# Attention scores in packed units of four blocks, one more half batch of x through the crossbar, and a longer wait for the loads

## Chip, core and metric

The kernel runs on one core of a Trainium2 chip. The metric is the time of one execution on the device, in microseconds (us); the median of several runs is given. A profile is one more execution, recorded by the hardware profiler; its span runs from the first instruction to the last.

## What is computed

Two parts follow each other. First an attention with 4 batches, 8 heads, 768 positions and 64 elements a head: each position attends to the first 8 positions and to the 96 positions up to itself, with a penalty that grows with the distance (a slope for each head). Then a feed-forward layer over the 4 x 768 = 3072 tokens with 512 features: a product with `w_in` (512 x 2048), a squared ReLU, a product with `w_out` (2048 x 512).

```python
scores = scale * (q @ k.T) - slope[h] * dist          # only kept positions
a = exp(scores - max) ; a = a / sum(a)
x = (a @ v), heads side by side -> [3072, 512]
out = (relu(x @ w_in) ** 2) @ w_out
```

Since only 8 + 96 positions are kept, a tile of 128 queries needs two blocks of 128 keys at most: its own tile, and a "before" block. In the before block the first 32 key rows are replaced by those of tile 0, so that the global positions are in it (`kb` for keys, `vb` for values, both copied together on the chip). The weights exp(score) are multiplied by a mask that holds exp(-slope * distance), or 0; the sum comes from a column of ones at the end of v.

## The kernel before

**Tiles and halves.** A batch has 6 tiles of 128 queries. Work goes by half batches (`hb` 0 to 7) of three tiles: `half` 0 holds tiles 0 to 2, `half` 1 tiles 3 to 5. Heads go in pairs (`NPAIR` = 4): the two heads of a pair lie on partitions 0-63 and 64-127, so their score matmuls (L453, 64 rows each) run side by side. The first two half batches (the opening) are handled tile by tile in an order written out by hand; their code is touched only in which buffers they share.

**Stages.** From then on TensorE works through stages, one for each half batch: stage `hb` runs the feed-forward of half batch `hb` as *main* work (layer 1: 16 jobs of 4 matmuls, L563; layer 2: 12 jobs of 4 matmuls, L612; 28 in all) and slips in the attention of half batch `hb` + 1 as *side* work. Stage 1 is shorter: its main work is 18 layer-2 jobs. `merge` puts each side job ahead of the main job with the number that it is given.

**Attention of a half batch, before.** For each pair of heads `a`: `score` (one job, 10 or 12 matmuls into four PSUM banks of 384 or 256 columns: `GROUPS`, two banks for each head), exponentials on ScalarE (L468), products with the mask on VectorE (L480, L484) into `phat`, then `attend` (L508, phat times v into PSUM bank `av`), normalization on VectorE (L515, L517) into `tm`, and the transpose of `tm` into `xt`, the input of layer 1. For half batch 2, q and k are turned by TensorE (`turn`, L400) and x too (`to_x`, L532, with an eviction on ScalarE or VectorE). For half batches 3 to 7 q, k (`turn_by_dma`, L418) and x (`to_x_by_dma`, L544) are transposed by crossbar DMAs that SP issues.

**Banks.** [...] Six (`ps_big`) serve scores, layer 1 and layer 2 in turn, two (`ps_att`) attention outputs and transposes.

**Order.** A planner (`Plan.run`) fixes the order of the instructions on each engine before the kernel runs, from costs and latencies written in the code. TensorE's jobs keep the order in which they were listed, the loads keep theirs, and the rest goes by the planned time. On the chip each engine then takes its list strictly in order: an instruction that waits holds up what stands behind it.

**Loads.** q, k and v come from memory by DMAs that POOL issues (L310), in one list: q, k, v of a half batch, three tiles each. The q load of half batch `hb` > 3 waits for the q and k transposes of half batches `hb` - 2 (their staging buffers become free) and `hb` - 1 (so that loads and those transposes don't meet). The q and k transposes of a half batch wait for its last k load.

```python
before = (prev.turned if prev else []) + (halves[x.hb - 1].turned if x.hb > 3 else [])
```

Of the kernel before, what the change touches and what calls it, by code (L numbers as in the profile page):

```python
# [25 lines left out]
LOADING = """v1 k1 v0 q1 k2 q2 k3 v2 k4 q3 q4 c0 k5 q5 v3 c1 v4 c2 c3 v5"""  # L26

# [121 lines left out]
def kernel(  # L149
# [150 lines left out]
    def list_loads(x):  # L300
        r0 = x.half * HALF
        prev = halves[x.hb - 2] if x.hb >= 2 else None
        before = (prev.turned if prev else []) + (halves[x.hb - 1].turned if x.hb > 3 else [])
        vbefore = [halves[x.hb - x.half - 3].attended[-1]] if x.hb >= 4 else []

        def rows(src, name, t, rank=None):
            def emit(e):
# [4 lines left out]
                if x.hb > 3 and name == "sq" and t == 0:  # L312
                    for turn in halves[x.hb - 1].turns:
                        behind(dma, turn)
# [98 lines left out]
    def turn_by_dma(x):  # L413
# [16 lines left out]
    GROUPS = {  # L430
        0: ([(0, 0), (1, 0), (1, 1)], [(2, 0), (2, 1)]),
        1: ([(3, 0), (4, 0), (5, 0)], [(3, 1), (4, 1), (5, 1)]),
    }

    def score(x, a, only=None):
        groups = GROUPS[x.half]
        st, weighs = x.phat.setdefault(a, ({}, []))
        mine = [g for g in range(2) if only in (None, g)]

        def emit(e):  # L440
            bt = x.bt
            for g in mine:
                blocks = groups[g]
                st[g] = pair = [ps_big.tile([P, 512], FP32, name="sp", tag="big")
                                for _ in range(2)]
                if g == mine[0]:
                    warm(pair[0])
                for i, (r, before) in enumerate(blocks):
                    for h in range(2):
                        rows = slice(h * D, (h + 1) * D)  # L450
                        lhsT = (bt.kb[rows, a, r - 2, :] if before and r > 1
                                else bt.qk[rows, 1, r - before, a, :])
                        nc.tensor.matmul(pair[h][:, i * P:(i + 1) * P], lhsT=lhsT,  # L453
                                         rhs=bt.qk[rows, 0, r, a, :],
                                         start=True, stop=True)
        n_mm = sum(len(groups[g]) for g in mine)
        job = plan.pe(0.182 + 0.062 * n_mm, emit, x.qk_ops[a], [big] * 2 * len(mine))

        for i, g in enumerate(mine):
            blocks = groups[g]  # L460
            n = len(blocks) * P
            c0 = 3 * P * g
            exps = []
            for h in range(2):
                def ex(e, g=g, h=h, n=n):
                    if h == 0:
                        st["ex", g] = phat_p.tile([P, 2, 3 * P], FP16, name="ex", tag="ex", bufs=6)
# [55 lines left out]
    def to_x(x, a):  # L523
        st, norm = x.tm[a]

        def emit(e):
            if x.xt is None:
                x.xt = h_p.tile([P, NCT, HALF], FP16, name="xt", tag="xt")
# [373 lines left out]
```

## Time and profile before

| what | value |
|---|---|
| median of 5 runs | 218.9 us (218.71, 218.89, 218.90, 219.59, 219.90) |
| the profiled execution: its time, its span | 219.5 us, 217.7 us |
| busy: TensorE, ScalarE, VectorE | 96%, 58%, 54% of the span |
| score matmuls L453 | 264, in 24 jobs |
| attention matmuls L508 | 264, in 24 jobs |
| transposes of x on TensorE L532 | 12 |
| crossbar transposes of x L544 | 20 |
| granted TensorE clock | 0.999 of full speed |

How to read it: in rows of groups, a line of the code, the engine, the operation, `out<-in` by the program's names, shapes, the number of instructions; then busy time, the mean of one in ns, and the idle time just before them with what ended it. In a timeline a row is start, length (both us), engine, line and operation; idle time in brackets. PE is TensorE, PEld its weight loads, DVE VectorE, ACT ScalarE, POOL GpSimd, SP SyncE; SPq and POOLq are the queues of these engines that issue DMAs. `hps` is layer 1's sum, `yps` layer 2's, `sp` the scores, `av` the attention output, `ex` the exponentials, `hr` the relu and `h` its square. The ends of matmuls are modelled, so the starts are what counts.

### The profile page before, as it was taken

The numbers are of one execution on the slowest core, as the hardware profiler recorded it, in microseconds if no ns is written. First come the engines' busy times: TensorE is split into PE (matmuls) and PEld (weight loads), VectorE is DVE, ScalarE is ACT, GpSimd is POOL, SyncE is SP. The second block draws the span as 40 slices with busy tenths as digits, with TensorE's granted clock in tenths as the row PEclk, the third lists the DMA queues.
The fourth block names the chain that finished last, engine by engine and source line by source line (L and its number), as shares of the span: only waits on it lengthen the run. The fifth ranks groups of instructions, "written<-read, shape, count | busy, mean of one in ns | idle before, by whom it ended". The sixth has DMA issues, their size and how long they took to land.

```text
span 217.7 us, 4847 instructions
## 1 busy us (share of the span) xinstructions
PE 210.1 (96%) x1917; PEld 127.8 (59%) x1917; DVE 117.5 (54%) x339; ACT 127.1 (58%) x286; POOL 68.2 (31%) x84
## 2 busy tenths in 40 slices
PE   6998999999999999999999999999999999999993
PEld 7776899755555565446554565446644565455552
DVE  7488887434764298317952488308850488114300
ACT  7689986744662788139831787149821885137421
POOL 8996534486049019204900193000000000000000
PEclk9999999999999999999999999999999999999999
DMA  7999999999999979997994899673103101220012
GB/s 117 150 159 179 196 200 207 168 154 173 97 205 159 174 186 103 145 201 133 126 132 121 188 94 144 105 147 96 39 20 114 53 18 36 69 96 0 3 52 93
DMA packets 106727, 26.41 MB, mean 121 GB/s; under 512 B 99408, under 2 KB 103760, under 8 KB 106704
## 3 DMA queue, kind: packets, MB, share of 16 engines
q0 software_dynamic: 77024, 13.37, 84.5%
q1 hardware_dynamic: 28640, 12.46, 24.8%
q10 hardware_dynamic: 1040, 0.26, 0.5%
q8 instruction: 15, 0.25, 0.5%
q14 instruction: 8, 0.07, 0.1%
HBM read 27.26 MB, written 6.29 MB: 154 GB/s over the span
## 4 chain that ended last, share of the span: by engine, by line
PE 74%; DMA 12%; POOL 10%; issue 1%; DVE 1%; ACT 0%; SPq 0%; POOLq 0%
PE hps L563 36%; PE yps L612 27%; DMA v<-in_v_dram 6%; POOL sk L310 4%; PE av L508 4%; DMA w_in_sb<-in_moe_w_in_dram 4%; POOL sq L310 4%; PE sp L453 3%; POOL v L310 2%; DMA qk<-sk 2%; PE yps L640 2%; PE av L740 1%; PE sp L701 1%; PE trx L767 0%; DVE phat L484 0%
## 5 line engine op out<-in xcount | busy, mean ns | idle before, releaser
L563 PE MATMUL hps<-xt,w_in_sb 128*128 128x384 f16 (+2 forms) x608 | 89.1, 301 | 0.6 <-DMA w_in_sb<-in_moe_w_in_dram 0.6
L612 PE MATMUL yps<-w_out_sb,h 128*128 128x512 f16 x368 | 83.0, 379 | 0.0
L563 PEld LDWEIGHTS <-w_in_sb 128*128 128x128 f16 x608 | 53.7, 98 | 27.3 <-DMA w_in_sb<-in_moe_w_in_dram 0.8
L598 DVE TENSOR_TENSOR h<-hr 128x768 f16<-128x768 f16 (+1 forms) x70 | 36.1, 521 | 52.5 <-ACT hr L587 52.1
L587 ACT ACTIVATE hr<-hps 128x384 f16<-128x384 f32 (+1 forms) x110 | 55.5, 514 | 14.8 <-PE hps L563 11.8
L612 PEld LDWEIGHTS <-h 128*128 128x128 f16 x368 | 35.1, 98 | 39.4
L198 ACT COPY y<-yps 128x512 f32<-128x512 f32 (+1 forms) x25 | 14.3, 570 | 62.8 <-PE yps L612 60.3
L468 ACT ACTIVATE ex<-sp 128x384 f16<-128x384 f32 x96 | 36.7, 477 | 1.5 <-PE sp L453 1.4
L310 POOL DMA_DIRECT2D sq<-in_q_dram x23 | 20.4, 895 | 52.3 <-DMA qk<-sq 28.2
L310 POOL DMA_DIRECT2D v<-in_v_dram x24 | 21.8, 934 | 5.6 <-DMA w_out_sb<-in_moe_w_out_dram 3.3
L310 POOL DMA_DIRECT2D sk<-in_k_dram x23 | 20.5, 906 | 3.7 <-DMA w_out_sb<-in_moe_w_out_dram 2.9
L517 DVE TENSOR_TENSOR tm<-av,rec 128x384 f16<-128x384 f32 x24 | 13.4, 557 | 0.8
L200 DVE COPY vb<-v 128x520 f16<-128x520 f16 (+1 forms) x32 | 10.2, 321 | 5.6 <-DMA v<-in_v_dram 5.1
L515 DVE RECIPROCAL rec<-av 128x6 f32<-128x6 f32 x24 | 4.7, 196 | 14.8 <-PE av L508 14.5
L508 PEld LDWEIGHTS <-phat 128*128 128x128 f16 x264 | 10.0, 98 | 3.8 <-DVE phat L484 0.6
L484 DVE TENSOR_TENSOR phat<-ex,mask 128x768 f16<-128x768 f16 x24 | 12.2, 550 | 0.0
L508 PE MATMUL av<-v,phat 128*128 128x65 f16 x168 | 11.5, 194 | 0.0
L200 DVE COPY kb<-qk 128x96 f16<-128x96 f16 (+4 forms) x56 | 11.0, 266 | 0.8 <-DMA qk<-sk 0.5
L480 DVE TENSOR_TENSOR phat<-ex,mask 128x768 f16<-128x768 f16 (+1 forms) x24 | 10.6, 485 | 0.1
L508 PE MATMUL av<-vb,phat 128*128 128x65 f16 x96 | 10.2, 194 | 0.3 <-DVE phat L484 0.3
L453 PE MATMUL sp<-qk 64*128 64x128 f16 x168 | 8.9, 219 | 0.0
L200 DVE COPY qk<-trp 128x512 f16<-128x512 f16 (+1 forms) x11 | 4.3, 398 | 8.3 <-PE trp L400 4.8
(65 smaller groups left out, 135.3 us busy)
## 6 DMA issues: line engine op xcount, KB each, us to landing
out_dram<-y SPq DMA_DIRECT2D x23, 256.0 KB, 2.3
v<-in_v_dram POOLq DMA_DIRECT2D x24, 128.0 KB, 6.6
sk<-in_k_dram POOLq DMA_DIRECT2D x23, 128.0 KB, 5.8
sq<-in_q_dram POOLq DMA_DIRECT2D x23, 128.0 KB, 5.6
w_in_sb<-in_moe_w_in_dram POOLq DMA_DIRECT2D x4, 512.0 KB, 10.9
w_out_sb<-in_moe_w_out_dram POOLq DMA_DIRECT2D x4, 512.0 KB, 15.8
xt<-tm SPq DMA_TRANSPOSE x20, 3.1
rsk<-in_k_dram ACTq DMA_DIRECT2D x1, 256.0 KB, 4.3
```

Of the source, the lines that this page charges most:

```text
L198: nc.scalar.copy(out=out, in_=in_)
L200: eng(e).tensor_copy(out=out, in_=in_)
L310: dma = nc.gpsimd.dma_start(out=dst, in_=src[x.b, :, r0 + t * P:r0 + (t + 1) * P, :] .rearrange("h p d -> p h d"))
L453: nc.tensor.matmul(pair[h][:, i * P:(i + 1) * P], lhsT=lhsT, rhs=bt.qk[rows, 0, r, a, :], start=True, stop=True)
L468: nc.scalar.activation(out=st["ex", g][:, h, 0:n], in_=st[g][h][:, 0:n], func=AF.Exp, scale=scale)
L484: eng(e).tensor_tensor(out=phat[:, :, c0:c0 + n].rearrange("p e (i c) -> p e i c", c=P), in0=ex[:, :, 0:n].rearrange("p e (i c) -> p e i c ...
L508: nc.tensor.matmul(av[:, h, j, :], lhsT=phat[:, h, c * P:(c + 1) * P], rhs=rhs, start=n == 0, stop=n == len(mine) - 1)
L517: nc.vector.tensor_tensor(out=st["tm"].rearrange("p t e d -> p e t d"), in0=av[:, :, :, 0:D], in1=rec[:, :, :, None].to_broadcast([P, 2, H ...
L563: nc.tensor.matmul(st["ps"][:, i * n:(i + 1) * n], lhsT=w_in_sb[:, kk, m * P:(m + 1) * P], rhs=x.xt[:, kk, c0:c1], start=kk == 0, stop=kk ...
L587: nc.scalar.activation(out=o, in_=i, func=AF.Relu)
L598: eng(e).tensor_tensor(out=x.h2[:, m0:m0 + width, c0:c1], in0=hr, in1=hr, op=ALU.mult)
L612: nc.tensor.matmul(st["ps"], lhsT=x.h2[:, m, j * P:(j + 1) * P], rhs=w_out_sb[:, m, :], start=m == 0, stop=m == NFT - 1)
```

## The change

1. *Scores in units of four blocks.* A block is (pair of heads, tile, own or before). Four blocks of one head side fill a whole PSUM bank (4 x 128 columns), so a unit takes two banks and two exponentials of 512 columns. An even half batch has 5 units: one for each pair (tiles 1 and 2, own and before), and one with tile 0 of all four pairs, whose product goes into a tile of its own (`phat0`). An odd one has 24 blocks in a row, cut into 6 units, so a unit can reach over two pairs. `TOGETHER` joins the units into three TensorE jobs of two units (the last of an even half batch: one). The weights lie as `phat[pair][head, tile, own|before]`.
2. *Places.* `PLACES` names the main job ahead of which each side job goes: three score jobs, four attend jobs, and for half batch 2 its four `turn` jobs. Scores now begin at place 0, ahead of the first layer-1 job, where before the fractions gave place 2; `merge` takes the numbers as they are.
3. *x of half batch 2 by crossbar.* `to_x` is gone, and `to_x_by_dma` serves every half batch from 2 on. It also records its DMAs in `x.turns`.
4. *Loads.* The loads of half batch `hb` > 3 wait also for the last x transpose of half batch `hb` - 2.
5. The opening's `ex` and `ph0` tiles share buffers with those of the later half batches.

```diff
@@ -24,6 +24,12 @@
 
 
...
+PLACES = {2: (3, 7, 7, 7, 10, 11, 12, 1, 0, 1, 0),
+          0: (0, 4, 9, 6, 11, 16, 18), 1: (0, 6, 11, 9, 11, 17, 19)}
 
 
 class Op:
@@ -300,7 +306,7 @@
     def list_loads(x):
         r0 = x.half * HALF
         prev = halves[x.hb - 2] if x.hb >= 2 else None
-        before = (prev.turned if prev else []) + (halves[x.hb - 1].turned if x.hb > 3 else [])
+        before = (prev.turned if prev else []) + ([*halves[x.hb - 1].turned, prev.x_ops[NPAIR - 1]] if x.hb > 3 else [])
         vbefore = [halves[x.hb - x.half - 3].attended[-1]] if x.hb >= 4 else []
 
         def rows(src, name, t, rank=None):
@@ -310,7 +316,7 @@
                 dma = nc.gpsimd.dma_start(out=dst, in_=src[x.b, :, r0 + t * P:r0 + (t + 1) * P, :]
                                           .rearrange("h p d -> p h d"))
                 if x.hb > 3 and name == "sq" and t == 0:
-                    for turn in halves[x.hb - 1].turns:
+                    for turn in halves[x.hb - 1].turns + halves[x.hb - 2].turns[-1:]:
                         behind(dma, turn)
                 if name == "sk":
                     x.last_load = dma
@@ -427,87 +433,90 @@
         for a in range(NPAIR):
             x.qk_ops[a] = x.turned + [plan.add(*fix_k(x, a), x.turned[:1], wait=4.0)]
 
-    GROUPS = {
-        0: ([(0, 0), (1, 0), (1, 1)], [(2, 0), (2, 1)]),
-        1: ([(3, 0), (4, 0), (5, 0)], [(3, 1), (4, 1), (5, 1)]),
-    }
-
-    def score(x, a, only=None):
-        groups = GROUPS[x.half]
-        st, weighs = x.phat.setdefault(a, ({}, []))
-        mine = [g for g in range(2) if only in (None, g)]
-
-        def emit(e):
-            bt = x.bt
-            for g in mine:
-                blocks = groups[g]
-                st[g] = pair = [ps_big.tile([P, 512], FP32, name="sp", tag="big")
-                                for _ in range(2)]
-                if g == mine[0]:
-                    warm(pair[0])
-                for i, (r, before) in enumerate(blocks):
+    UNITS = [[[(a, r, bf) for r in range(1, HT) for bf in (False, True)] for a in range(NPAIR)]
+             + [[(a, 0, False) for a in range(NPAIR)]]]
+    seq = [(a, r, bf) for a in range(NPAIR) for r in range(HT, NT) for bf in (False, True)]
+    UNITS.append([seq[i:i + 4] for i in range(0, len(seq), 4)])
+    TOGETHER = [[[0, NPAIR], [1, 2], [3]], [[0, 1], [2, 3], [4, 5]]]
+
+    def score(x, k):
+        bt = x.bt
+        units = [UNITS[x.half][u] for u in TOGETHER[x.half][k]]
+        sp = {}
+
+        def emit(e):
+            for u, unit in enumerate(units):
+                sp[u] = [ps_big.tile([P, 4, P], FP32, name="sp", tag="big") for _ in range(2)]
+                if u == 0:
+                    warm(sp[u][0].rearrange("p i c -> p (i c)"))
+                for i, (a, r, before) in enumerate(unit):
                     for h in range(2):
                         rows = slice(h * D, (h + 1) * D)
                         lhsT = (bt.kb[rows, a, r - 2, :] if before and r > 1
                                 else bt.qk[rows, 1, r - before, a, :])
-                        nc.tensor.matmul(pair[h][:, i * P:(i + 1) * P], lhsT=lhsT,
-                                         rhs=bt.qk[rows, 0, r, a, :],
-                                         start=True, stop=True)
-        n_mm = sum(len(groups[g]) for g in mine)
-        job = plan.pe(0.182 + 0.062 * n_mm, emit, x.qk_ops[a], [big] * 2 * len(mine))
-
...
-            weighs.append(plan.add({"DVE": 0.06 + n * 0.0011}, weigh,
-                                   exps + [mask_ops[2 * a], mask_ops[2 * a + 1]]))
+                        nc.tensor.matmul(sp[u][h][:, i, :], lhsT=lhsT,
+                                         rhs=bt.qk[rows, 0, r, a, :], start=True, stop=True)
+        pairs = sorted({a for unit in units for a, _, _ in unit})
+        job = plan.pe(0.182 + 0.062 * 4 * len(units), emit,
+                      [o for a in pairs for o in x.qk_ops[a]], [big] * 2 * len(units))
+        for u, unit in enumerate(units):
+            weigh_unit(x, unit, job, u, sp)
+
+    def weigh_unit(x, unit, job, u, sp):
+        st = {}
+        exps = []
+        for h in range(2):
+            def exp(e, h=h):
+                if h == 0:
+                    st["ex"] = phat_p.tile([P, 2, 4, P], FP16, name="ex", tag="ex", bufs=6)
+                nc.scalar.activation(out=st["ex"][:, h], in_=sp[u][h], func=AF.Exp, scale=scale)
+            exps.append(plan.add({"ACT": 0.505}, exp, [job] + exps))
+            job.users[2 * u + h].append(exps[-1])
+        if unit[0][1] == 0:
+            def weigh(e):
+                x.phat0 = phat_p.tile([P, 2, NPAIR, P], FP16, name="ph0", tag="ph0")
+                eng(e).tensor_tensor(
+                    out=x.phat0, in0=st["ex"], op=ALU.mult,
+                    in1=mask[:, :, 0:P].rearrange("p (a h) c -> p h a c", h=2))
+            op = plan.add({"DVE": 0.62}, weigh, exps + mask_ops)
+            for a in range(NPAIR):
+                x.weighs[a].append(op)
+            return
+        for a in sorted({a for a, _, _ in unit}):
+            mine = [(i, r) for i, (b, r, _) in enumerate(unit) if b == a][::2]
+            i0, n, t0 = mine[0][0], len(mine), mine[0][1] % HT
+
+            def weigh(e, a=a, i0=i0, n=n, t0=t0):
+                if a not in x.phat:
+                    x.phat[a] = phat_p.tile([P, 2, HT, 2 * P], FP16, name="phat", tag="phat")
+                eng(e).tensor_tensor(
+                    out=x.phat[a][:, :, t0:t0 + n], op=ALU.mult,
+                    in0=st["ex"][:, :, i0:i0 + 2 * n].rearrange("p e (t b) c -> p e t (b c)", b=2),
+                    in1=mask[:, 2 * a:2 * a + 2, None, P:3 * P].to_broadcast([P, 2, n, 2 * P]))
+            x.weighs[a].append(plan.add({"DVE": 0.06 + n * 0.28}, weigh,
+                                        exps + mask_ops[2 * a:2 * a + 2]))
 
     def attend(x, a):
         bt = x.bt
-        st, weighs = x.phat[a]
-        where = [(3 * g + i, r, bf) for g, blocks in enumerate(GROUPS[x.half])
-                 for i, (r, bf) in enumerate(blocks)]
-
-        def emit(e):
-            phat = st["phat"]
+        st = {}
+        blocks = [(j, bf) for j in range(HT) for bf in (False, True) if x.half or j or not bf]
+
+        def emit(e):
             st["av"] = av = ps_att.tile([P, 2, HT, D + 1], FP32, name="av", tag="att")
             warm(av.rearrange("p e t d -> p (e t d)"))
             for h in range(2):
-                for j in range(HT):
+                for j, before in blocks:
                     r = x.half * HT + j
-                    mine = [(c, bf) for c, rr, bf in where if rr == r]
-                    for n, (c, before) in enumerate(mine):
-                        rhs = (bt.vb[:, r - 2, 2 * a + h, :] if before and r > 1
-                               else bt.v[:, r - before, 2 * a + h, :])
-                        nc.tensor.matmul(av[:, h, j, :], lhsT=phat[:, h, c * P:(c + 1) * P],
-                                         rhs=rhs, start=n == 0, stop=n == len(mine) - 1)
-        job = plan.pe(0.0305 * 2 * len(where), emit, weighs + x.v_in + [bt.vb_ops[t] for t in range(*tiles_before(x))], [att])
+                    rhs = (bt.vb[:, r - 2, 2 * a + h, :] if before and r > 1
+                           else bt.v[:, r - before, 2 * a + h, :])
+                    lhsT = (x.phat[a][:, h, j, before * P:(before + 1) * P] if r
+                            else x.phat0[:, h, a, :])
+                    nc.tensor.matmul(av[:, h, j, :], lhsT=lhsT, rhs=rhs, start=not before,
+                                     stop=before or r == 0)
+        job = plan.pe(0.0305 * 2 * len(blocks), emit, x.weighs[a] + x.v_in
+                      + [bt.vb_ops[t] for t in range(*tiles_before(x))], [att])
 
         def norm(e):
             av = st["av"]
@@ -520,30 +529,15 @@
         x.attended.append(job)
         x.tm[a] = (st, plan.after(job, {"DVE": 0.74}, norm))
 
-    def to_x(x, a):
+    def to_x_by_dma(x, a):
         st, norm = x.tm[a]
 
         def emit(e):
             if x.xt is None:
                 x.xt = h_p.tile([P, NCT, HALF], FP16, name="xt", tag="xt")
-            st["trx"] = ps_att.tile([P, HT, P], FP16, name="trx", tag="att")
-            warm(st["trx"].rearrange("p t c -> p (t c)"))
-            for t in range(HT):
-                nc.tensor.transpose(out=st["trx"][:, t, :], in_=st["tm"][:, t, :, :],
-                                    identity=ident)
-        job = plan.pe(3 * 0.056, emit, [norm], [att])
-        x.x_ops[a] = plan.after(job, {"ACT": 0.39, "DVE": 0.31}, lambda e: copy(
-            e, x.xt[:, a, :], st["trx"].rearrange("p t c -> p (t c)")))
-
-    def to_x_by_dma(x, a):
-        st, norm = x.tm[a]
-
-        def emit(e):
-            if x.xt is None:
-                x.xt = h_p.tile([P, NCT, HALF], FP16, name="xt", tag="xt")
-            nc.sync.dma_start_transpose(
+            x.turns.append(nc.sync.dma_start_transpose(
                 out=x.xt[:, a, :].rearrange("p (t c) -> p t c", c=P),
-                in_=st["tm"].rearrange("p t e d -> p (t e d)"))
+                in_=st["tm"].rearrange("p t e d -> p (t e d)")))
         x.x_ops[a] = plan.add({"SP": 1.2}, emit, [norm])
         x.x_ops[a].lag = 2.5
 
@@ -650,6 +644,7 @@
 
     for x in halves:
         x.turned, x.turns, x.attended = [], [], []
+        x.weighs = [[] for _ in range(NPAIR)]
         x.qk_ops, x.phat, x.tm, x.x_ops, x.h2_ops, x.l1, x.l2 = {}, {}, {}, {}, {}, {}, {}
         x.xt = x.h2 = None
 
@@ -705,12 +700,12 @@
             needs += [kb_ops[r - 1]] if r > 1 else tile_ops[r - 1]
         job = plan.pe(0.182 + NPAIR * 0.07 + added * H * 0.056, emit, needs, [big] * 2)
         exps = []
-        st["ph", before] = phat_p.tile([P, 2, NPAIR, P], FP16, name="ph0", tag="ph0", bufs=4)
+        st["ph", before] = phat_p.tile([P, 2, NPAIR, P], FP16, name="ph0", tag="ph0")
         for h in range(2):
             def ex(e, h=h):
                 if h == 0 and not added:
-                    st["ex", before] = phat_p.tile([P, 2, NPAIR, P], FP16, name="ex0", tag="ex0",
-                                                   bufs=3)
+                    st["ex", before] = phat_p.tile([P, 2, NPAIR, P], FP16, name="ex", tag="ex",
+                                                   bufs=6)
                 nc.scalar.activation(out=st["ph" if added else "ex", before][:, h],
                                      in_=st["sp", before][h], func=AF.Exp, scale=scale)
             exps.append(plan.add({"ACT": 0.51}, ex, [job] + exps))
@@ -775,21 +770,19 @@
 
     def attention(x):
         jobs = []
-        early = x.hb > 2
+        places = PLACES[x.hb if x.hb == 2 else x.half]
+        for k in range(len(TOGETHER[x.half])):
+            jobs.append((places[k], lambda k=k: score(x, k)))
         for a in range(NPAIR):
-            at = 0.04 + 0.16 * a if early else 0.1 + 0.17 * a
-            jobs.append((at, lambda a=a: score(x, a)))
-            jobs.append((at + 0.17, lambda a=a: attend(x, a)))
-            if early:
-                jobs.append((at + 0.17, lambda a=a: to_x_by_dma(x, a)))
-            else:
-                jobs.append((0.04 * a, lambda a=a: turn(x, a)))
-                jobs.append((at + 0.3, lambda a=a: to_x(x, a)))
+            if x.hb == 2:
+                jobs.append((places[7 + a], lambda a=a: turn(x, a)))
+            jobs.append((places[3 + a], lambda a=a: attend(x, a)))
+            jobs.append((places[3 + a], lambda a=a: to_x_by_dma(x, a)))
         return sorted(jobs, key=lambda j: j[0])
 
     def merge(main, side):
         for i, f in enumerate(main):
-            while side and side[0][0] * len(main) <= i:
+            while side and side[0][0] <= i:
                 side.pop(0)[1]()
             f()
         for _, g in side:
```

## The prediction

> **What bounds the kernel now.** I read the page from its busy shares to the chain that ended last, then that chain in order of time, then the order of instructions where TensorE waits. The page first:
>
> ```profile
> PE 210.1 (96%) x1917; PEld 127.8 (59%) x1917; DVE 117.5 (54%) x339; ACT 127.1 (58%) x286; POOL 68.2 (31%) x84
> ...
> PE 74%; DMA 12%; POOL 10%; issue 1%; DVE 1%; ACT 0%; SPq 0%; POOLq 0%
> ```
>
> TensorE is the only full engine. The DMA and POOL shares of the chain lie ahead of 77 us; from there to the end the chain is TensorE alone. So after the opening the end moves by what TensorE issues less, plus or minus what it waits. Busy time can't tell this (its ends are modelled); starts can. The chain in order of time gives each kind of work its price (start, length, what):
>
> ```profile
> 96.72 1.30 PE hps L563 x8
> 98.02 0.39 PE sp L453 x10
> 98.41 2.71 PE hps L563 x16
> ...
> 105.55 0.41 PE av L508 x10
> 105.96 2.60 PE hps L563 x16
> ...
> 113.46 0.31 PE av L508 x10
> 121.97 0.44 PE sp L453 x12
> ```
>
> Sixteen matmuls of layer 1 take 2.60 us (0.1625 each), but 2.71 straight after a score job; ten attention matmuls take 0.31, but 0.41 straight after one. So leaving the scores costs 0.10. Entering costs the same: starts of two L563 matmuls lie 0.162 apart, from the last L563 to the first L453 it is 0.258, and from the last L453 to what follows 0.148 where a pair of heads takes 0.0565. That is 0.096 in, 0.096 out: **0.192 us per group of score matmuls, whatever its size**.
>
> From the starts of layer 1 (71.60, 96.56, 120.51, 144.92, 168.86, 193.27) the stages last 24.96, 23.95, 24.41, 23.95 and 24.41 us. Odd half batches (12 score matmuls a pair of heads) cost 24.41, even ones 23.95; the first is 0.55 too long. The timeline there shows why:
>
> ```profile
> 75.56 0.62 DVE L200 COPY vb<-v 128x520 f16<-128x520 f16 x2 [1.38 <-DMA v<-in_v_dram]
> 76.10 1.01 DVE L484 TENSOR_TENSOR phat<-ex,mask 128x768 f16<-128x768 f16 x2
> 76.14 0.34 PE L453 MATMUL sp<-qk 64*128 64x128 f16 x6
> ...
> 76.70 0.20 PE L508 MATMUL av<-v,phat 128*128 128x65 f16 x1
> 77.04 0.59 DVE L200 COPY vb<-v 128x520 f16<-128x520 f16 x2
> 77.16 0.20 PE L508 MATMUL av<-vb,phat 128*128 128x65 f16 x1 [0.26 <-DVE phat L484]
> ```
>
> VectorE stood 1.38 us at a copy that waits for v of half batch 4; the weights for TensorE's next job were queued behind it. By starts TensorE lost 0.11 + 0.44 = 0.55. Nothing else after 34 us is more than rounding.
>
> **The change part by part.** *Fewer score groups.* Before: four jobs for each of half batches 2 to 7, 24 groups. After: three for each of 3 to 7; for half batch 2 the second and third stand back to back at place 7, so two. 24 − (15 + 2) = 7 groups × 0.192 = −1.34 us (0.38 of it before half batch 2's layer 1). Score matmuls stay 264, attention matmuls 264. A rule of the Trainium skill bears on this: TensorEngine Tiling (Array Packing), "Tiling Modes", says changing the tiling mode drains TensorE, without a figure. TensorE: Matmul & The Clock Gate, "Single matmul latency", puts the constant of an isolated warm matmul at 166 ns; an estimate with that at each of 14 switches is −2.3. The row has the duration itself, so I take −1.34.
>
> *x of half batch 2 by crossbar.* Twelve transposes on TensorE go; four of three took 0.167 each (starts 0.056 apart): −0.67. Four evictions (0.48 on ScalarE or 0.36 on VectorE) go too, beside TensorE. Added are four crossbar transposes, 1.18 us each on SP's queue, behind half batch 3's two q and k transposes (on SP from 56.3 to 60.6, not moved); the first x is ready at 61.8, so SP is free. Half batch 2's attention also moves: last attend job six layer-2 jobs (0.863 each, 4 × 0.216) ahead of the end. From its last matmul: 0.22 to the reciprocal, up to 0.9 for two kb copies and an earlier normalization in VectorE's queue, 0.75 for its own, then the flight. What each flight took:
>
> ```profile
> L544 SPq DMA_TRANSPOSE xt<-tm x7: 1178/1179/2141, 155.2 to 187.4; - x7
> DMA to landing us min/median/max: 2.3/2.3/3.2
> ```
>
> Without loads beside it, 2.3; in the windows 102 to 111 and 126 to 136 us, beside loads, the medians are 5.6 and 5.8, at most 6.3. Here the loads wait, so 2.3: 4.2 us in all, against 5.2 + 0.64 (the score job now ahead of layer 1) = 5.8. Hidden, 1.6 to spare. With 6.3 it would be 2.4 late. A rule that speaks against the new wait of the loads: DMA: Bandwidth & Descriptors, "Rules for kernel authors", says a transpose beside ordinary DMAs needs nothing (it speaks of correctness). With the page's fixed part of about 2.0 us ("Anatomy of one DMA", for the other kind of queue) and its 261 GB/s for transposes ("Latency and other measured facts") an estimate for these 96 KB is 2.4 us, loads or not, and the wait buys nothing. The rows say 2.3 and 5.8: just here it decides.
>
> *The wait of the loads.* Behind POOL's waiting load stand all nine loads of that half batch, behind them its two transposes on SP, and the x transposes queued behind those. Half batch 4's loads start when half batch 2's x has landed, near 70, not 62.9. Rows: last sk landed 10.4 after the first issue, last v 13.6. So sk 80.4, transposes (1.5 each on SP, 4.1 to landing) by 87, v by 83.6; needed at 95.5 and, in VectorE's queue (vb now stands behind the third normalization), at 86. Later ones: loads of 5, 6, 7 near 91, 113, 139, their q and k by 107, 129, 155, needed at 119, 143, 167. All hidden by 8 us or more; v by 2 or more. So 0, and with vb moved the **0.55 wait should go**: −0.55 (between −0.55 and 0 for the loads' part).
>
> *Packing.* Activations of 384 take 502 ns, of 512 619; in a run they start 0.371 and 0.49 apart, so 16 × 0.371 = 5.9 becomes 12 × 0.49 = 5.9: nothing, and ScalarE is hidden anyway (13.9 of 24.4 us). Products with the mask keep their elements. VectorE gets three more relus a stage, 3 × 0.55, near 12 of layer 1's 13.7 us: close, so my bound for it is 0 to 0.2 a stage.
>
> *A new wait.* In the order of the changed kernel the two score jobs at place 7 take six PSUM banks while layer 2's sum holds one of the six. The sixth (unit 3, second head) is the bank that unit 1's first head got 0.5 us before. So TensorE stands in the group until that block is exponentiated. From the group's start S: fourth pair S + 0.27; activation 0.25 later (57.540 to 57.792 in the trace) at 0.52; 0.62 long, to 1.14; 0.12 back to TensorE (22.427 to 22.549) = 1.26. It would have started at 0.55: **+0.71**. Bounds: 0 (the bank is another), 1.3 (a 0.59 eviction gets ahead on ScalarE). No other reuse came out tight: at a stage's start the third layer-1 job needs the first block's bank at 1.94, free at 1.5.
>
> Sum: −1.34 − 0.67 − 0.55 + 0.71 = **−1.85** on the profiled execution: 219.5 → 217.65 (span 217.7 → 215.9, 1.8 around it). That execution is 0.6 above the median of 218.9. Runs at 218.7 to 218.9 probably had less of the 0.55 wait, and can't win it again: 218.9 − 1.30 = 217.6; with all of it 217.05. I predict **217.4**.
>
> **Rivals.** *No stall at place 7*: the banks fall otherwise or ScalarE is quicker. For it: nothing in the trace. 217.4 − 0.71 = 216.7. *VectorE or ScalarE become the bound at a stage's start*, where the scores now come first, four banks at once ahead of layer 1, and evictions wait in line: 0.2 for each of five stages eats the −0.96 of those, 218.4. For it: VectorE's 12 of 13.7; against it: before also took four banks a job, with shorter gaps. *Slower: half batch 2's x comes late*. The last transpose is the last link of attend, normalization, SP, flight, and layer 1's first matmul needs it. At a flight of 6.3, the longest beside loads, it is 2.4 late: 219.8. It passes 218.9 from a flight of 5.4, if some loads still run or SP stands at another transfer. Against it: the wait is put ahead of just these loads. *It doesn't do what it says*, that is the groups still switch as often: only the −0.67 and stall remain, about 218.9.
>
> **How the numbers follow.** Chances: main 0.58, no stall 0.10, bound at the stage's start 0.17, late x 0.09, no fewer switches 0.06. A measurement here tells about 0.3% (0.66 us) from no change, so faster means under 218.24. Main and the first rival are faster, of the second three in five, of late x a quarter (a shorter flight): 0.58 + 0.10 + 0.10 + 0.02 = 0.80. Same: the rest of the second, the last, some late x: 0.07 + 0.05 + 0.01 = 0.13; slower 0.07. The range reaches from no stall (216.6) to the second rival (218.5).
>
> **What would show it.** Right: 17 score groups in place of 24 in the later stages, no L532 transposes of x, layer-1 starts about 24.2 and 23.75 apart, the stage of half batch 2's layer 1 without its 0.55; a gap of about 0.7 inside the score matmuls near 60 us, released by ScalarE; x landing in about 2.3; POOL's loads starting 7 to 15 us later with nobody waiting. Wrong: gaps of TensorE ahead of layer 1 released by a DMA of xt, or by relus on VectorE in each stage; a wait at vb in VectorE's queue; no gap at 60.

## The result

The changed kernel takes 217.25 us (median of 20 runs, 216.68 to 218.85), the kernel before 218.88 in the same comparison (39 runs). The ratio is 0.9925, 95% interval 0.9908 to 0.9941: 1.6 us less. The profiled execution took 217.38 us, with a span of 215.6, at a granted clock of 0.999; before it was 219.5 and 217.7. Times and ratios leave out slow executions, those over 1.5% above the fastest of the same kernel: one of six in the first experiment below, four of 20 in the second.

The page of the changed kernel, its busy shares and the chain that ended last:

```profile
PE 208.5 (97%) x1905; PEld 127.7 (59%) x1905; DVE 121.0 (56%) x340; ACT 119.8 (56%) x242; POOL 68.3 (32%) x84
...
PE 88%; POOL 5%; DMA 4%; ACT 2%; DVE 0%; issue 0%; POOLq 0%
```

Twelve matmul instructions fewer (the transposes of x), and a chain that is 88% TensorE instead of 74%. VectorE has 121.0 us instead of 117.5 and did not become a bound. The chain in order of time (start, length, what):

```profile
51.32 0.37 DVE qk L206
...
51.71 1.25 ACT qk L204 x3
...
53.00 0.49 PE trp L406 x6
53.49 1.73 PE yps L606 x8
55.22 0.55 PE sp L459 x16
55.77 3.56 PE yps L606 x16
59.33 0.34 PE sp L459 x7
...
59.70 0.61 ACT ex L474
...
60.35 0.38 PE sp L459 x7
60.73 0.41 PE av L516 x10
...
95.74 0.55 PE sp L459 x16
96.30 2.71 PE hps L557 x16
99.00 0.55 PE sp L459 x16
```

Read it from the top: after the opening TensorE leaves the chain twice. At 51.3 to 53.0 the turns of q and k wait for evictions (`qk`), one on VectorE (L206) and three on ScalarE (L204); at 59.7 the scores wait for an exponential on ScalarE (L474). From there to the last eviction nothing but TensorE follows. From 95.74 on one sees the pattern of the later stages: 16 score matmuls in one group of 0.55 us ahead of layer 1's first job. The waits say the same from the other side (what waited, for what: us in total, times, longest):

```profile
POOL sq L316 <- DMA xt<-tm: 64.7, 4, 18.5
...
DVE vb L206 <- DMA v<-in_v_dram: 1.4, 2, 1.1
...
PE sp L459 <- ACT ex L474: 0.4, 1, 0.4
...
PE trp L406 <- ACT qk L204: 0.2, 1, 0.2
```

Waits of TensorE are counted here from modelled ends; by starts the two are 0.62 and 0.35. POOL's loads wait 64.7 us for the crossbar transposes; the first of them, for half batch 4, looks like this:

```profile
71.39 2.62 POOL L316 DMA_DIRECT2D sq<-in_q_dram  x3 [18.48 <-DMA xt<-tm]
```

No computing engine waits for these loads in turn. SP's queue does, with the transposes of q and k (20.8 us for k's loads, 11.7 for q's), and no engine waits for those. The two waits of `vb` in the table lie in the opening, ahead of 30 us. The copy of `vb` that stood 1.38 us in VectorE's queue before is now a row without a wait:

```profile
86.15 0.56 DVE L526 TENSOR_TENSOR tm<-av,rec 128x384 f16<-128x384 f32 x1
86.62 0.60 DVE L206 COPY vb<-v 128x520 f16<-128x520 f16 x2
```

And the four transposes of half batch 2's x, in the window from 60 to 77 us, landed in 2.4 us at the median:

```profile
L538 SPq DMA_TRANSPOSE xt<-tm x4: 1197/1206/2147, 62.0 to 68.4; - x4
DMA to landing us min/median/max: 2.3/2.4/3.3
```

**A clean measure.** The opening differs from execution to execution by about a microsecond. So I compare each trace from its own first `turn` matmul of half batch 2 (at 50 to 51.5 us) to its last matmul, by starts. Before: 50.87 to 213.96, which is 163.10 us. After: 50.78 to 212.13, which is 161.35 us. A second profile of the changed kernel gave 161.35 again. The difference is −1.75 us, and it comes apart into five pieces that are read from starts: seven groups of scores fewer (−1.50, see below), 12 transposes (−0.67), the wait at `vb` (−0.55), a new wait in the scores at 59.72 (0.622 between two starts that are otherwise 0.003 apart: +0.62), and a new wait in the turns at 52.59 (0.407 where 0.056 is usual: +0.35). Sum −1.75.

**The end.** The stretch leaves out what follows the last matmul, and that became shorter too. The span ends 3.77 us after the start of the last matmul before, 3.47 after. The last eviction shows it, in a span of 217.7 us before and of 215.6 after:

```profile
214.27 0.37 ACT L198 COPY y<-yps 128x256 f32<-128x256 f32 x1 [1.38 <-PE yps L640]
...
212.44 0.37 ACT L204 COPY y<-yps 128x256 f32<-128x256 f32 x1 [1.38 <-PE yps L634]
```

The last store lands equally soon in both, 2.42 and 2.39 us after the start of the last matmul. Then SP goes through the rest of a closing list of nine semaphore waits, about 0.06 us each: eight are left in the kernel before, four in the changed kernel, whose last store stands further down that list. The three traces with half batch 2's x turned on TensorE have 3.75 to 3.77 us here, the ten with it on the crossbar 3.46 to 3.50. So −0.30 came along with the transposes, without anyone having planned it. With −0.09 in the opening, the two spans differ by 2.14 us.

### The profile page after: what moved, and what is told of

It is laid out like the page before. It is cut to its first block, busy times and chain, and to the rows that moved or that the text cites. A ratio compares the mean times of both kernels' runs of the same rounds, so it can differ in the third digit from the quotient of the medians.

```text
span 215.6 us, 4772 instructions
## 1 busy us (share of the span) xinstructions
PE 208.5 (97%) x1905; PEld 127.7 (59%) x1905; DVE 121.0 (56%) x340; ACT 119.8 (56%) x242; POOL 68.3 (32%) x84
## 4 chain that ended last, share of the span: by engine, by line
PE 88%; POOL 5%; DMA 4%; ACT 2%; DVE 0%; issue 0%; POOLq 0%
PE hps L557 39%; PE yps L606 36%; PE sp L459 4%; PE av L516 4%; DMA w_in_sb<-in_moe_w_in_dram 4%; POOL sq L316 2%; POOL sk L316 2%; PE yps L634 2%; POOL v L316 1%; PE av L735 1%; ACT qk L204 1%; PE trp L406 0%; PE trx L762 0%; PE sp L696 0%; ACT ex L474 0%
## 5 line engine op out<-in xcount | busy, mean ns | idle before, releaser
L581 ACT ACTIVATE hr<-hps 128x384 f16<-128x384 f32 (+1 forms) x97 | 49.6, 512 | 18.0 <-PE hps L557 15.2
L204 ACT COPY y<-yps 128x512 f32<-128x512 f32 (+1 forms) x25 | 14.2, 569 | 67.1 <-PE yps L606 61.0
L592 DVE TENSOR_TENSOR h<-hr 128x768 f16<-128x768 f16 (+1 forms) x70 | 35.6, 520 | 24.7 <-ACT hr L581 24.5
L316 POOL DMA_DIRECT2D sq<-in_q_dram x23 | 20.5, 901 | 68.5 <-DMA xt<-tm 64.7
L583 DVE TENSOR_SCALAR hr<-hps 128x384 f16<-128x384 f32 x25 | 13.9, 556 | 37.9 <-PE hps L557 37.0
L474 ACT ACTIVATE ex<-sp 128x512 f16<-128x512 f32 x66 | 34.1, 610 | 1.2 <-PE sp L459 1.2
L494 DVE TENSOR_TENSOR phat<-ex,mask 128x1024 f16<-128x1024 f16 (+1 forms) x36 | 19.9, 595 | 1.9 <-ACT ex L474 1.9
L206 DVE COPY vb<-v 128x520 f16<-128x520 f16 (+1 forms) x32 | 10.2, 320 | 2.0 <-DMA v<-in_v_dram 1.4
L516 PE MATMUL av<-v,phat 128*128 128x65 f16 x144 | 10.9, 194 | 0.0
L459 PEld LDWEIGHTS <-qk 64*128 64x128 f16 x168 | 6.3, 94 | 6.7 <-issue 6.3
L459 PE MATMUL sp<-qk 64*128 64x128 f16 x168 | 9.8, 218 | 0.4 <-ACT ex L474 0.4
L206 DVE COPY kb<-qk 128x96 f16<-128x96 f16 (+4 forms) x56 | 9.0, 226 | 0.3
L206 DVE COPY qk<-trp 128x512 f16<-128x512 f16 (+1 forms) x10 | 3.9, 402 | 7.6 <-PE trp L406 4.4
```

Source lines behind the costliest of these rows:

```text
L204: nc.scalar.copy(out=out, in_=in_)
L206: eng(e).tensor_copy(out=out, in_=in_)
L316: dma = nc.gpsimd.dma_start(out=dst, in_=src[x.b, :, r0 + t * P:r0 + (t + 1) * P, :] .rearrange("h p d -> p h d"))
L459: nc.tensor.matmul(sp[u][h][:, i, :], lhsT=lhsT, rhs=bt.qk[rows, 0, r, a, :], start=True, stop=True)
L474: nc.scalar.activation(out=st["ex"][:, h], in_=sp[u][h], func=AF.Exp, scale=scale)
L494: eng(e).tensor_tensor(out=x.phat[a][:, :, t0:t0 + n], op=ALU.mult, in0=st["ex"][:, :, i0:i0 + 2 * n].rearrange("p e (t b) c -> p e t (b c ...
```

## Experiments

All ratios are to the kernel before; times are medians. "Stretch" is the measure just described, from the first turn to the last matmul: 161.35 us for the changed kernel, 163.10 for the one before.

### Is the longer wait of the loads needed?

The first kernel takes the wait away, for all half batches.

```diff
-        before = (prev.turned if prev else []) + ([*halves[x.hb - 1].turned, prev.x_ops[NPAIR - 1]] if x.hb > 3 else [])
+        before = (prev.turned if prev else []) + (halves[x.hb - 1].turned if x.hb > 3 else [])
...
-                    for turn in halves[x.hb - 1].turns + halves[x.hb - 2].turns[-1:]:
+                    for turn in halves[x.hb - 1].turns:
```

> The changed kernel without its longer wait of the loads: the loads of half batch 4 wait only for q and k's transposes, as before the change, and start near 62 us instead of 70. My theory (a crossbar transpose beside loads takes 5 to 6.3 us instead of 2.3): the transposes of half batch 2's x fly beside those loads, the last one lands 1.5 to 2.4 us too late, layer 1 of stage 2 waits for it, 218.8 to 219.6 us. The other theory (the loads cost the transpose nothing, the wait buys nothing): flights stay at 2.3 to 3, no gap of TensorE ahead of layer 1, 217.25 us. In between, flights of 4 us would eat the 1.6 us to spare and no more: 217.25 with longer flights in the profile.

Measured: 222.86 us, ratio 1.0157 (1.0113 to 1.0201); stretch 167.61, +6.26. The side is mine, the size is neither: more than twice what I expected. The transposes of x, 60 to 80 us:

```profile
L538 SPq DMA_TRANSPOSE xt<-tm x4: 1185/1236/1886, 62.5 to 68.6; - x4
...
  PE hps L557: 4.2, 2
...
DMA to landing us min/median/max: 4.4/8.1/9.0
```

They are issued at the same times as in the changed kernel (62.5 to 68.6 against 62.0 to 68.4), so neither SP nor the attention is late. But they fly 4.4 to 9.0 us instead of 2.3 to 3.3, and layer 1 waits twice (the row of PE). By starts these two are 2.43 and 2.14 us, and the second matmul came 0.15 late for the second x: 4.72 together, where the stage became 6.25 longer. The rest, 1.53, is in the clock. In a table by time (length; busy time of PE, PEld, DVE, ACT, POOL; then PE's granted clock, DMA share, GB/s):

```profile
75.00:77.00 2.00, 0.32 (x1) 0.10 (x1) 0.00 (x0) 0.00 (x0) 0.00 (x0) 1.00 1.69 206
77.00:78.00 1.00, 0.34 (x2) 0.17 (x2) 0.00 (x0) 0.00 (x0) 0.00 (x0) 0.71 2.12 167
78.00:79.00 1.00, 1.00 (x5) 0.49 (x4) 0.56 (x1) 0.00 (x0) 0.00 (x0) 0.50 0.62 105
...
81.00:82.00 1.00, 1.00 (x8) 0.61 (x7) 0.76 (x2) 0.71 (x2) 0.00 (x0) 1.00 0.87 176
```

After nearly 5 us with one matmul in them, layer 1 runs at clock 0.50, its matmuls 0.32 apart instead of 0.162, from 77.4 to 80.8. The Trainium skill, TensorE: Matmul & The Clock Gate, Part 1, has this rule: about 3.4 us of idleness halve the clock, and about as long a busy time brings it back. The return after 3.4 us fits. The halving goes further than the rule: no idle stretch here was that long, only 2.43 and 2.14 us with a single matmul between them. My price of a late x had left the clock out. The profiled execution is 1.2 us above the median. One execution of this kernel, at a granted clock of 1.000, took 221.11, the others at 0.990 to 0.992 took 222.75 to 224.06; that this one kept its full clock through the gap is likely, but no trace shows it.

The later stages of this kernel last 23.73 and 24.20 us, as in the changed one. So only the wait of half batch 4's loads is worth anything; those of 5, 6 and 7 buy nothing.

The second kernel takes a smaller dose: the loads wait for the first x transpose, not the last.

```diff
-        before = (prev.turned if prev else []) + ([*halves[x.hb - 1].turned, prev.x_ops[NPAIR - 1]] if x.hb > 3 else [])
+        before = (prev.turned if prev else []) + ([*halves[x.hb - 1].turned, prev.x_ops[0]] if x.hb > 3 else [])
...
-                    for turn in halves[x.hb - 1].turns + halves[x.hb - 2].turns[-1:]:
+                    for turn in halves[x.hb - 1].turns + halves[x.hb - 2].turns[-NPAIR:][:1]:
```

> The changed kernel with the loads waiting for the first x transpose of half batch hb - 2 instead of the last: the loads of half batch 4 start near 65 us, after the first flight, beside the other three. My theory (what lengthens a flight is the loads' packets that are under way beside it): the first flight stays at 2.3 us, the next one near 3, the last two at 5 to 8, the last lands near 75 instead of 70.8, TensorE waits 2 to 4 us and then runs some matmuls at half clock: 219.5 to 222 us. Rival (only flights issued behind waiting or earlier loads suffer, or the first x alone was the critical one): 217.25 us.

Measured: 219.66 us, ratio 1.0031 (1.0008 to 1.0054), 2.2 above the changed kernel in the same comparison (217.47). The time is within what I expected, but the wait is shorter than 2 to 4 us and no half clock followed. In its profile:

```profile
L538 SPq DMA_TRANSPOSE xt<-tm x4: 1187/1206/1737, 62.8 to 68.7; - x4
...
  PE hps L557: 1.3, 1
...
DMA to landing us min/median/max: 2.3/5.5/5.9
```

The first flight, alone, 2.3; the other three 5.3, 5.6 and 5.9. TensorE waits once, 1.42 us by starts, and the stretch is 1.45 longer: in this profile the clock stayed at 1.00 there. The other 0.8 us of the 2.2 lie ahead of the first turn, where the edit changes nothing. The second flight was expected near 3 and took 5.3, although no load had been landing when it was issued. In the changed kernel the last x lands at 70.77, and the fourth matmul, which needs it, starts at 72.52: 1.75 us to spare. A last flight of 5.93 uses that up and, by this sum, 1.8 more; 1.42 was measured, because that transpose was issued 0.4 us earlier, counted from layer 1's start. So the wait is needed. That loads under way lengthen the flights is shown by these two kernels; by what means they do it is not.

### What does a group of scores cost?

Half batches 3 to 7 get 28 groups instead of 15, with the same units.

```diff
-          0: (0, 4, 9, 6, 11, 16, 18), 1: (0, 6, 11, 9, 11, 17, 19)}
+          0: (0, 1, 4, 5, 9, 6, 11, 16, 18), 1: (0, 1, 6, 7, 11, 12, 9, 11, 17, 19)}
...
+    SINGLE = [[[0], [NPAIR], [1], [2], [3]], [[0], [1], [2], [3], [4], [5]]]
+
+    def together(x):
+        return TOGETHER[0] if x.hb == 2 else SINGLE[x.half]
```

> The changed kernel with the score units of half batches 3 to 7 each a job of its own (5 or 6 jobs for each half batch instead of 3), at places of their own; the same units, matmuls, exponentials and places of attend. 28 groups instead of 15 there, 13 more. My theory (each group of score matmuls costs 0.192 us of TensorE, in and out, whatever its size): 13 x 0.192 = +2.5, 219.75 us, stages of about 24.6 and 24.3 us instead of 24.2 and 23.7. [...] Rival (switching is free, the gain of the change lay elsewhere): 217.25 us.

Measured: 220.01 us, ratio 1.0043 (1.0024 to 1.0062); stretch 164.12, +2.77. So the whole gain of the change, and more, is gone with its groups. 2.77 / 13 = 0.213 us for each group, where I had 0.192; the prediction's other price, 0.33 a group, would have made it +4.3. The starts show the rest: the first pair of a group takes 0.064 to the next where the others take 0.053, and the second layer-1 matmul after a group comes 0.174 after the first, not 0.162. With these, 0.258 + 0.148 − 0.162 − 0.053 + 0.011 + 0.012 = 0.214.

Why does it cost anything? The next kernel lets each score matmul use all 128 rows.

```diff
-                        rows = slice(h * D, (h + 1) * D)
+                        rows = slice(0, P)
```

> The changed kernel with each score matmul over all 128 rows instead of the 64 of its head: it sums over both heads of the pair, so the scores are other numbers, while blocks, banks, groups, exponentials and places are the same. Two matmuls that ran side by side then run one after the other: for half batches 2 to 7 about 132 more steps of 0.056 us (the distance of the transposes' starts), +7.4 us. My theory (a group costs its 0.19 to 0.21 us because the tiling of the array changes from 128 to 64 rows and back): the starts from layer 1 to a score fall from 0.258 to 0.162, from a score to layer 1 from 0.148 to 0.056, and 17 x 0.21 = 3.6 us are won back, 221.0 us. Rival (the cost is that of a change of bank, of operands or of accumulation, at any tiling): the starts stay at 0.258 and 0.148, 224.6 us.

Measured: 220.76 us, ratio 1.0073 (1.0049 to 1.0097); stretch 164.76, +3.42. By starts, from layer 1 to a score is now 0.162, from layer 2 to a score 0.216 (0.312 before), from a score to layer 1 0.056: the same as without a change of kind. The chain shows it without a count, since layer 1 takes its plain 3.90 and 1.95 us right after a group:

```profile
120.86 0.89 PE sp L459 x16
121.75 3.90 PE hps L557 x24
125.65 0.89 PE sp L459 x16
126.55 1.95 PE hps L557 x12
```

In the changed kernel the 24 after a group take 4.01 and the 12 take 2.06. So the toll belongs to the change between matmuls of 64 rows, two side by side, and matmuls of 128 rows. A group's change of banks or operands alone costs nothing. Whether the rows or the running side by side make the toll was not separated. The sum closes: 132 × 0.056 = +7.39, 17 × 0.214 = −3.64, and the wait at place 7 falls from 0.62 to 0.29, −0.33 (the slower group asks later): +3.42. (Running two heads side by side is still worth twice its toll, 7.39 against 3.64.)

### Is x by crossbar worth its twelve transposes?

```diff
-            jobs.append((places[3 + a], lambda a=a: to_x_by_dma(x, a)))
+            if x.hb == 2:
+                jobs.append((places[3 + a] + 2, lambda a=a: to_x(x, a)))
+            else:
+                jobs.append((places[3 + a], lambda a=a: to_x_by_dma(x, a)))
```

> The changed kernel with x of half batch 2 turned by TensorE again (12 transposes, and an eviction for each pair of heads), two places after its attend jobs; all other parts of the change stay. My theory (12 x 0.056 = 0.67 us of TensorE and nothing else, flights of the crossbar were hidden): 217.9 us. The loads of half batch 4 then start near 62 us again; if v's early arrival or a late copy of vb brings back a wait in VectorE's queue, up to 0.55 more, 218.5. Rival (the crossbar transposes were not wholly hidden, or the evictions cost as much again): 217.25 or less, and over 218.5.

Measured: 218.49 us, ratio 0.9978 (0.9958 to 0.9999); stretch 162.04, +0.70, which is the 0.67 and little else. The end is 3.75 us long again, 0.28 more than in the changed kernel: together 0.98. The medians are 1.24 apart, across two comparisons; the intervals allow both. The stage of half batch 2's layer 1 still lasts 24.20 us. The loads of half batch 4 were early here (from 62.1), so the wait at `vb` does not depend on them.

### Where did the wait at vb go?

In the kernel before, one number of the planner puts the copy of `vb` later in VectorE's list.

```diff
-                      wait=0.0 if bt is batches[0] else 4.0)
+                      wait=0.0 if bt is batches[0] else 8.0)
```

> The kernel before with one number of its planner changed: the copy of vb is planned 8 instead of 4 us after v's loads, so it stands behind the third normalization in VectorE's queue. My theory: TensorE's 0.55 us near 76.7 us go, at most 218.9 - 0.55 = 218.35 us; by my guess that most runs had less of that wait, 218.5 to 218.8. If the change's gain came wholly from groups and transposes: no gap in the profile to win back, 218.9.

Measured: 218.81 us, ratio 1.000 (0.998 to 1.002). In the profile the stage is 24.41 us long instead of 24.96, the 0.55 is gone, and the copies start at 79.52 without a wait, instead of at 75.56 and 77.04:

```profile
79.52 0.93 DVE L200 COPY vb<-v 128x520 f16<-128x520 f16 x2
```

The stretch is 162.68, only 0.42 less, because 0.12 came back at another attention job (56.66). So the order in VectorE's list alone makes or removes this wait. Whether most executions of the kernel before had it in full is not settled: the interval of the ratio just reaches 0.42 us, and the median is 0.3 below that of the kernel before in the same comparison (219.12).

### The two new waits of stage 1

Each has one number in `PLACES[2]`. First the third score job one place later:

```diff
-PLACES = {2: (3, 7, 7, 7, 10, 11, 12, 1, 0, 1, 0),
+PLACES = {2: (3, 7, 8, 7, 10, 11, 12, 1, 0, 1, 0),
```

> The changed kernel with the third score job of half batch 2 at place 8 instead of 7. My theory (the wait of 0.57 us inside the scores near 60 us comes from six banks being wanted back to back while layer 2's sum holds one): the wait goes, one more group comes, 217.25 - 0.57 + 0.21 = 216.9 us. Rival (ScalarE is behind by then, the wait only moves): 217.2 to 217.5 us.

Measured: 216.89 us, ratio 0.9915 (0.9888 to 0.9941). Stretch 160.94, −0.40: the 0.62 is gone and one group of 0.21 came. The wait was for a bank, as the theory has it.

Then one turn of q and k one place later:

```diff
-PLACES = {2: (3, 7, 7, 7, 10, 11, 12, 1, 0, 1, 0),
+PLACES = {2: (3, 7, 7, 7, 10, 11, 12, 1, 0, 2, 0),
```

> The changed kernel with one of the four turns of q and k of half batch 2 at place 2 instead of 1. My theory (the wait of 0.35 us near 52.6 us is TensorE, which has the turns back to back, ahead of ScalarE's evictions): it goes, 216.9 us. Rival (the same wait at the next turn): 217.25 us.

Measured: 216.87 us, ratio 0.9900 (0.9868 to 0.9933), which is as near to the changed kernel's ratio as the intervals can tell; stretch 161.35, exactly as without the edit. The wait at the turns is gone, and the same time is lost ten microseconds later:

```profile
62.35 1.28 DVE L494 TENSOR_TENSOR phat<-ex,mask 128x1024 f16<-128x1024 f16 x2
...
62.72 0.19 PE L516 MATMUL av<-v,ph 128*128 128x65 f16 x1
...
63.09 0.27 PE L516 MATMUL av<-v,phat 128*128 128x65 f16 x3 [0.17 <-DVE phat L494]
```

TensorE reaches the second attend job 0.34 us earlier and stands there for the product with the mask, which depends on the exponentials that were late at place 7. The median I expected came, but only by chance: the theory behind it failed. The rival was nearly right, only that the wait moved further than to the next turn. Both edits together:

```diff
-PLACES = {2: (3, 7, 7, 7, 10, 11, 12, 1, 0, 1, 0),
+PLACES = {2: (3, 7, 8, 7, 10, 11, 12, 1, 0, 2, 0),
```

> The changed kernel with two numbers changed for half batch 2: its third score job goes one place later, at 8 (so the two jobs no longer want six banks back to back), and one of the turns of q and k goes from place 1 to 2. My theory (the wait of 0.57 us inside the scores near 60 us is for a bank that an exponential holds, the 0.35 us near 52.6 is TensorE ahead of ScalarE's evictions of the turns): both go, one more group of scores costs 0.19: 217.25 - 0.57 - 0.35 + 0.19 = 216.5 us. Rival (ScalarE is short there, and the waits only move to the next place): 217.2 us.

Measured: 216.88 us, ratio 0.9895 (0.9864 to 0.9926); stretch 160.60, −0.75, with no wait of TensorE left in it. The chain has no ScalarE any more:

```profile
51.17 0.67 PE trp L406 x12
51.84 0.86 PE yps L606 x4
52.71 0.34 PE trp L406 x6
...
59.22 0.55 PE sp L459 x16
59.77 0.41 PE av L516 x10
60.19 0.86 PE yps L606 x4
61.05 0.33 PE sp L459 x8
```

The medians had not shown the 0.75, so the changed kernel and this one ran once more side by side.

> The changed kernel itself once more, so that the next run has it on the same chip and in the same rounds: 217.25 us as before, its two waits of TensorE (0.35 and 0.57 us) at the same places. If the half microsecond of the earlier comparison came from the chip of that day, it comes out nearer to 216.9.

> The kernel with the third score job at place 8 and one turn at place 2, beside the changed kernel: by the trace of its first run 0.75 us less from the first matmul of layer 1 to the last matmul, so 216.5 us if the changed kernel gives 217.25. Rival: opening and store at the end vary by as much, no difference to be told: within 0.3 us of the changed kernel.

Measured: 217.47 us (ratio 0.9918, 0.9887 to 0.9949) and 216.72 us (0.9884, 0.9847 to 0.9921): 0.75 apart, as in the traces, whose stretches were again 161.35 and 160.60. The two intervals of the ratios overlap, so the medians alone would not prove it; the trace, twice the same to 0.01 us, does. By the traces this version beats both kernels.

## Why the prediction was right, and where not

217.4 was predicted and 217.25 came. The sum of −1.85 stands against −1.75 in the stretch, but against −2.14 in the whole span, since the end gave 0.30 more. Step by step:

- *Score groups, −1.34.* 24 groups became 17, as predicted. Mechanism right, size too small: 0.214 each, together −1.50. I had taken the entry and the exit, and missed the slower first pair and the slower second matmul of layer 1. (The exit is 0.095, 0.148 less the 0.053 from pair to pair; with the 0.0565 that I named it would be 0.092.) Of the two prices I weighed, the row's (0.192) was near; the estimate from the latency of an isolated matmul (0.33 a group; TensorE: Matmul & The Clock Gate, Single matmul latency) was too high by half. The rule that a change of tiling mode drains TensorE (TensorEngine Tiling (Array Packing), Tiling Modes) agrees with the kernel with 128 rows, where the cost is gone; that it is a drain, no trace shows.
- *x of half batch 2 by crossbar, −0.67.* Right in the stretch: 0.70 by undoing it. That the end would be 0.30 shorter with it was not in the sum at all, and nothing in the argument pointed there: luck. The flights took 2.3 to 3.3, the last 2.35, and 1.75 us were left where I had 1.6.
- *The wait at vb, −0.55.* Gone, and the reason given, VectorE's list, is enough for it: moving the copy did the same in the kernel before, and loads that started early did not bring the wait back.
- *The bank at place 7, +0.71.* There, released by ScalarE, +0.62. The exponential started 0.43 after the group's start instead of 0.52, and TensorE went on 0.05 after its end instead of 0.12; TensorE also reached the place earlier, at 0.46 instead of 0.55.
- *"No other reuse came out tight."* This step failed. The turns' two banks were tight: at places 0 and 1 two turns each stand in a row, and the fourth waits until ScalarE has evicted the second, +0.35. It hid in the total because the groups brought 0.16 more than the sum had and the bank cost 0.09 less. That these errors nearly cancel, −1.75 for −1.85, is luck.
- *The loads' wait at nothing.* Right: the loads of half batch 4 were issued from 71.4 on, its v landed by 84.5, and `vb` was copied at 86.62 without standing.
- *The rival of a late x.* It did not happen, but its price was too low. I priced it with a flight of 6.3 us, the longest beside loads that the trace had: 2.4 late, 219.8. Without the wait of the loads the flights reached 9.0, and the halved clock came on top: 222.86. The skill's rule that a transpose beside ordinary DMAs needs nothing (DMA: Bandwidth & Descriptors, Rules for kernel authors) speaks of correctness and stands as that; taken for the time it would have been wrong by 5.6 us here.
- *VectorE or ScalarE as the bound.* Did not happen; the stages last 24.20 and 23.73 us, and no relu is waited for.
- *Where the median stands.* I placed it between −1.30 and −1.85 from 218.9 and it came at −1.6. The reason (that most runs had less of the 0.55) is not shown: the kernel before with `vb` later has a ratio of 1.000, with room for the whole 0.42 in its interval. The whole span of the profile fell by 2.14, so the point is nearer than its reason deserves.

## What to carry to other kernels

Where TensorE is full, count how often it changes between row-tiled and whole-array matmuls, not how many matmuls there are: 0.21 us a round trip, 1.50 in all, was the largest part of this gain. Before a transfer is moved onto the critical path, look at what else flies at that time: the same transpose took 2.3 us alone and up to 9 beside nine loads, and making the loads wait cost nothing because they had 2 to 8 us to spare. And after removing one wait, look in the trace for where the time is lost next: one of the two small fixes gave nothing until the other was made. And look at the end of the trace too: 0.3 us of this gain lay behind the landing of the last store.

## What was not expected of the hardware

- A crossbar transpose of 96 KB took 2.3 us alone. With the first load issued just after the second transpose, the second to fourth took 5.3 to 5.9. Issued 0.8 us behind the first load, one took 4.4, and three issued 3.7 to 7.0 us behind it took 7.4 to 9.0; the trace of before had shown 6.3 at most.
- Waits of 2.43 and 2.14 us with one matmul between them were followed by half clock for 3.4 us, which cost 1.5 us more; one wait of 1.42 us was not.
- After the last store had landed, SP's closing list of semaphore waits took about 0.06 us for each that was left: 0.3 us between eight and four of them.
- By starts, from the first turn to the last matmul, two executions of the same kernel agree within 0.01 us over 161 us (161.346 and 161.350, 160.596 and 160.597). Where the second pair differs, by 0.6 us, it is ahead of it, in the opening (first turn at 51.01 and 50.43).
